# The second expert layer as seven block products in three of five chunks, and its weight sums on VectorE

## The chip, the cores and the metric

The kernel runs on one core of a Trainium2 chip. The metric is device time in microseconds (us) of one execution. The core has a matrix engine (TensorE, PE in the profile; its weight loads are shown as PEld), three engines for elementwise work (VectorE or DVE, ScalarE or ACT, GpSimd or POOL) and SyncE (SP), which only issues transfers here. Each engine works through its own instructions in the order in which they were written out. Semaphores make one engine wait for another. SBUF is the working memory; PSUM, in eight banks, takes what TensorE writes, and an elementwise engine has to move ("evacuate") it from there.

## The reference

Two layers in a row. The first is a Fourier filter on each of 8 batches of 2496 tokens by 256 channels, with a soft threshold:

```
X = rfft(x, axis=1);  Yr = Xr @ w_r - Xi @ w_i + b_r;  Yi = Xr @ w_i + Xi @ w_r + b_i
Y = sign(Y) * max(|Y| - 0.01, 0)          (for Yr and Yi)
y = irfft(Yr + i*Yi, n=2496, axis=1)
```

The second is a mixture of experts, in which the mean over the tokens of a batch picks one of 8 experts for the whole batch:

```
e = argmax(mean(y, axis=1) @ w_gate);  g = softmax weight of e
h   = relu(y @ w1[e])                     256 -> 1024 features
out = g * (h @ w2[e])                     1024 -> 256
```

Inputs and result are in 32 bits, the kernel's matmuls in 16 bits with sums in 32 bits.

## The kernel before

**Stages of a batch.** The transform of length 2496 is done in two factors (39 and 64) with matmuls against tables. For batches 2 to 7 the steps are: the first factor (L812), evacuated to `A`, stored to HBM as `fwd` and read back in another layout as `XB`; then, in five groups q of four frequencies each, the second factor (L876) to `XT`, a sum of real and imaginary part on VectorE (`sm`, L895), three products with the filter's weights (L914, `T2`, `T1`, `T0` in PSUM), and the threshold on VectorE; then the inverse's first factor (L547) from `Y` to `V`, stored to HBM as `scr` and read back as `V2`, and its second factor (L1058), evacuated to `ysb`, the expert layer's input. Batches 0 and 1 use a direct form (`add_attn_direct`).

**The threshold on VectorE** is, in each group q: two instructions that write `tt` = `T2` + bias, one for the real and one for the imaginary part (L928); two that write `z` = `T1` or `T0` + `tt` (L937); a clamp `cl` (L946); and four that write `Y` = `z` - `cl` (L956), each with two inputs in SBUF. L547 waits for all four.

**The expert layer** of a batch goes over five chunks of tokens: four of 512 and one of 448 (batch 0 has its own cut). In each chunk the first layer takes 8 x 2 matmuls of 512 columns (L1391), each pair evacuated with the relu to `hs` by ScalarE or VectorE (L1404, L1406). The second layer has two forms.
- *Plain* (L1440): for each of two tiles of 256 tokens 16 matmuls of 256 columns, 32 for a chunk; one evacuation of 512 elements for each tile, scaled by g, to `ost` (L1457 or L1460); a store.
- *Seven products* (`add_fast`, L1203): the chunk's 512 tokens are halved (t), and so are the 1024 features (k) and the 256 outputs (h). A product of two-by-two blocks, which takes eight block products, is made of seven block products (`p1` to `p7`), with sums of blocks before and after. Four sums of `hs` blocks go to `S`, or back into `hs` (L1221 to L1231, VectorE); four differences of `w2` blocks, `T`, are made once for each batch (L1193 to L1196, "weight sums"); each product is 8 matmuls of 128 columns (L1254), 56 in all. They build up in two PSUM banks, `E` and `F`. Between the products four evacuations of 256 elements take what `E` holds (`take`, L1269 on ScalarE or L1272 on VectorE), and three instructions on VectorE add what `F` holds to an `ost` block (`add`, L1278). `S` has one buffer, `hs` two, `T` one, `ost` four. `p5`, `p6`, `p7` and `p4` read `T[0]` to `T[3]`.

A set `FAST` (L394) says which chunks take the second form: four chunks of the last batch, and the fourth chunk of batches 1 to 6. The weight sums run on POOL for batches 1 to 6 and on VectorE for batch 7. The last chunk, of 448 tokens, has a second part with turned operands (L1325) and stores issued by POOL (L1362).

**What sets the order.** The kernel registers operations with a planner (`Schedule`, L136): an engine, a planned occupation and latency in us, a due time, what they depend on, which buffers they take. `run` (L197) then writes them out one by one: of those that could start it picks the one with the earliest planned start, then the earliest due time. Evacuations (`S.evac`) may go to ScalarE or VectorE, whichever the plan has free first. So a change of one operation's engine or length changes the order of all engines behind it, and the order is fixed before the kernel runs. TensorE gets work of two batches mixed: the expert layer of batch b beside the filter of batch b + 1 or b + 2.

**Queues.** SP issues the stores and the transfers over HBM; POOL issues the loads of the inputs (`xin`, L306 and L310) and of the chosen expert's weights (`w1s` L1150, `w2s` L1155, two buffers each), in its own order with the weight sums.

Of the kernel before, what the change touches and what calls it, by code (L numbers as in the profile page):

```python
# [10 lines left out]
FP16 = mybir.dt.float16  # L11
# [5 lines left out]
P = 128  # L17
B = 8
N = 2496
D = 256  # L20
E = 8
F = 1024
# [226 lines left out]
def kernel(  # L249
# [12 lines left out]
    nc = tc.nc  # L262
# [8 lines left out]
    def pool(name, bufs, **kw):  # L271
        return ctx.enter_context(tc.tile_pool(name=name, bufs=bufs, **kw))
# [21 lines left out]
    spool = pool("sp", 1)  # L294
# [72 lines left out]
    bias = cpool.tile([P, 2, D], FP32, name="bias")  # L367
# [17 lines left out]
    S = Schedule(BANKS)  # L385
    xin_t, V2_t, ysb_t, A_t, XB_t, fwd_t, scr_t = ({} for _ in range(7))
    gbc_t, w1s_t, w2s_t = {}, {}, {}
# [3 lines left out]
    W_LATE, B_LATE = 46.0, 53.5  # L391
    WARM, COLD, WARM_END = 60, 12, 11.9
    LATE = -0.12
    FAST = {(B - 1, c) for c in range(4)} | {(b, c) for b in range(1, B - 1) for c in (3,)}  # L394
    PERIOD, SPAN, SHIFT = 49.5, 1.4, 0.6

    ps = psum.tile([P, 8, 512], FP32, name="ps")
# [2 lines left out]
    def bank(tag):  # L400
        return ps[:, BASE[tag] + S.bank[tag]]
# [75 lines left out]
    c1, c2, c3 = ([S.fixed(t)] for t in X0_AT[1:])  # L477
# [319 lines left out]
    def add_attn(b):  # L797

        vt = vt_of(b)
# [4 lines left out]
        for gp in range(NG // 2):  # L804
            tk = S.tok("a", BANKS["a"])
            cell = {}

            def mm(_, gp=gp, cell=cell):
                if gp == 0:
# [6 lines left out]
                     deps=[xd[min(gp // 4, len(xd) - 1)]],  # L816
                     after=m if gp else None,
                     allocs=[tk] if gp else [tk, Ak])
# [11 lines left out]
        for i, (g0, g1) in enumerate(((0, 6), (6, 12), (12, 18), (18, 21))):  # L830
            def wr_(_, g0=g0, g1=g1):
# [6 lines left out]
                if g1 == 21:  # L838
# [5 lines left out]
                              deps=a_ops[g0 // 2 : (g1 + 1) // 2],  # L844
# [4 lines left out]
        for q in range(NQ):  # L849
            def rd(_, q=q):  # L850
                if b not in XB_t:
# [4 lines left out]
                              allocs=[] if q else [Bk]))  # L856

        v_ops = []
        for q in range(NQ):
            f = 0.1 + 0.7 * q / NQ  # L860
            cell = {}
# [3 lines left out]
            for ch in range(2):  # L865
                tk = S.tok("a", BANKS["a"])
                hc = {}

                def mm(_, q=q, ch=ch, cell=cell, hc=hc):
# [4 lines left out]
                    for i in range(4):  # L874
# [5 lines left out]
                         allocs=[tk] if ch else [tk, Xk])  # L880
# [19 lines left out]
            m_ops, toks = {}, {}  # L900
            zk, Yk = S.tok("z", BUFS["z"]), S.tok("Y", BUFS["z"])
            for t in (2, 1, 0):
                tk = S.tok("a", BANKS["a"])
                toks[t] = tk

                def mm(_, t=t, cell=cell):
# [5 lines left out]
                    for a in range(2):  # L912
                        for ch in range(2):
# [7 lines left out]
                                deps=([so] if t == 2 else [m_ops[2]]) + w_in + [w_late],  # L921
                                allocs=[tk, zk, Yk] if t == 2 else [tk])
                Xk.rel.append(m_ops[t])

            z_ops = []
            for r in range(2):
                def t1(_, r=r, cell=cell):
                    nc.vector.tensor_add(  # L928
                        out=cell["tt"][:, r], in0=cell["T", 2].rearrange(
                            "p (a c) -> p a c", a=2),  # L930
                        in1=bias[:, r].unsqueeze(1).to_broadcast([P, 2, D]))
                o1 = S.op("DVE", 0.61, t1, vt(f + 0.03), deps=[m_ops[2]],
                          lat=0.74)
                toks[2].rel.append(o1)

                def z_(_, r=r, cell=cell):
                    nc.vector.tensor_add(  # L937
                        out=cell["z"][:, r], in0=cell["T", 1 - r].rearrange(
                            "p (a c) -> p a c", a=2), in1=cell["tt"][:, r])
                o2 = S.op("DVE", 0.61, z_, vt(f + 0.03), lat=0.74,  # L940
                          deps=[o1, m_ops[1 - r]])
                toks[1 - r].rel.append(o2)
                z_ops.append(o2)
# [242 lines left out]
    def add_weight_sums(b, w, wk, v):  # L1186
        tk = S.tok("T", 1)

        def ts(_):
            T_t[b] = T = spool.tile([P, 4, 4, P], FP16, name="T")  # L1190
            w2 = w2s_t[b].rearrange("p (k i) (h c) -> p k h i c", k=2, h=2)
            sub = (nc.gpsimd if b < B - 1 else nc.vector).tensor_sub
            sub(out=T[:, 0], in0=w2[:, 0, 1], in1=w2[:, 0, 0])  # L1193
            sub(out=T[:, 1], in0=w2[:, 1, 1], in1=T[:, 0])
            sub(out=T[:, 2], in0=w2[:, 1, 1], in1=w2[:, 0, 1])
            sub(out=T[:, 3], in0=w2[:, 1, 0], in1=T[:, 1])  # L1196
        p = b < B - 1
        t = S.op("POOL" if p else "DVE", 4.5 if p else 1.4, ts, v, deps=[w],
                 lat=4.7 if p else 1.5, allocs=[tk])
        wk.rel.append(t)  # L1200
        return t, tk

    def add_fast(b, c, ns, nl, cell, h_ops, hk, wk, tt, gb_op, v0):  # L1203
        t_op, t_tok = tt
        th, m = nl // 2, nl // 4
        tag = "o" if b < B - 1 else "ho"[c % 2]
        sk = S.tok("S", 1)
# [2 lines left out]
        vt = lambda x: v0 + PERIOD * (c * 8 + 8 + x) / 44  # L1210
# [22 lines left out]
        o1 = s_op("s1", 0, s1, vt(0), h_ops, [sk])  # L1233
        o2 = s_op("s2", 0, s2, vt(0.1), [o1])
        o3 = s_op("s3", 0, s3, vt(0.2), [o1])
# [8 lines left out]
        w2 = lambda k, h: lambda f: w2s_t[b][:, 4 * k + f, P * h : P * h + P]  # L1244
        T = lambda i: lambda f: T_t[b][:, i, f]

        def prod(x, dst, a, bb, start, deps, allocs=(), after=None):
            def mm(_):
                if start:
                    fc[dst[0]] = bank(tag).rearrange(  # L1250
                        "p (h i c) -> p h i c", h=2, i=2)
                for t in range(2):
                    for f in range(4):
                        nc.tensor.matmul(  # L1254
                            fc[dst[0]][0:m, dst[1], t, :], A[a](f, t), bb(f),
                            start=start and t == 0 and f == 0,
                            stop=f == 3,
                            skip_group_check=True)
            return S.mm([P] * 8, mm, vt(x), deps=deps, allocs=allocs, after=after)
# [23 lines left out]
        p1 = prod(0, ("E", 0), "11", w2(0, 0), True, h_ops[:4], [ek])  # L1283
        c1 = take(0.1, 0, 0, [p1, gb_op])
        p2 = prod(1.2, ("F", 0), "12", w2(1, 0), True, h_ops, [fk], p1)
        p5 = prod(2.4, ("F", 1), "S1", T(0), False, [o1, t_op], after=p2)
        a11 = add(2.5, 0, 0, 0, [p5, c1])
        p6 = prod(3.6, ("E", 0), "S2", T(1), False, [o2, c1], after=p5)
        u2 = take(3.7, 0, 1, [p6])
        p7 = prod(4.8, ("E", 0), "S3", T(2), False, [o3, u2], after=p6)  # L1290
        u3 = take(4.9, 1, 1, [p7])
        a22 = add(5.0, 1, 1, 1, [u3, p5, a11])
        p4 = prod(6.0, ("E", 0), "22", T(3), False, [u3], after=p7)
        c21 = take(6.1, 1, 0, [p4])
        p3 = prod(7.2, ("F", 1), "S4", w2(1, 1), False, [o4, a22], after=p4)
        a12 = add(7.3, 0, 1, 1, [p3, u2])
# [14 lines left out]
    T_t = {}  # L1311
# [56 lines left out]
    def add_moe(b, y_ops, yk, gate):  # L1368
        w, gb_op, wk = gate
        v0 = b * PERIOD  # L1370
        if any(x == b for x, _ in FAST):
            t_op = add_weight_sums(b, w, wk, v0 - 0.05 * PERIOD)
        for c, (ns, nl, tiles) in enumerate(NCH0 if b == 0 else NCH):
            x = ns / 64
            hk = S.tok("hs", BUFS["hs"])
            cell = {}
            h_ops = []
            for fc in range(E):
                v = v0 + PERIOD * (x + fc * nl / 512) / 44
                tag = "h" if b < B - 1 else "a"  # L1380
                tk = S.tok(tag, BANKS[tag])
                hc = {}

                def mm(_, fc=fc, ns=ns, nl=nl, cell=cell, hc=hc, tag=tag):
                    if fc == 0:
                        cell["hs"] = hpool.tile([P, E, 512], FP16, name="hs")
                    hc["p"] = ph = bank(tag)

                    w1v = w1s_t[b].rearrange("p h (t f i) -> p h t f i", t=2, i=4)
                    for ch in range(2):  # L1390
                        nc.tensor.matmul(  # L1391
                            ph[:, 0:nl], w1v[:, ch, fc // 4, :, fc % 4],
                            ysb_t[b][:, ch, ns : ns + nl],
                            start=(ch == 0), stop=(ch == 1))
                need = y_ops[: Y_NEED[ns // YB]] if b == 0 else y_ops
                m = S.mm([nl, nl], mm, v, deps=need + [w], after=m if fc else None,
                         allocs=[tk] if fc else [tk, hk])
                yk.rel.append(m)
                wk.rel.append(m)

                def ev(eng, fc=fc, nl=nl, cell=cell, hc=hc):
                    o, i = cell["hs"][:, fc, 0:nl], hc["p"][:, 0:nl]
                    if eng == "ACT":
                        nc.scalar.activation(out=o, in_=i, func=AFT.Relu)  # L1404
                    else:
                        nc.vector.tensor_scalar_max(out=o, in0=i, scalar1=0.0)  # L1406
                e = S.evac(nl, ev, v, deps=[m])
                tk.rel.append(e)
                h_ops.append(e)
            if (b, c) in FAST:  # L1410
                add_fast(b, c, ns, nl, cell, h_ops, hk, wk, t_op, gb_op, v0)
                continue
            for sp, tile_s in enumerate(tiles):
# [11 lines left out]
                for q in range(4):  # L1425
                    if q // 2 >= tile_s[1]:
                        break
                    v = v0 + PERIOD * (x + 6 * nl / 512 + 4 * sp + q) / 44

                    def mm(_, tile_s=tile_s, q=q, cell=cell, oc=oc, tag=tago,  # L1430
# [8 lines left out]
                        for ft in range(4 * (q % 2), 4 * (q % 2) + 4):  # L1439
# [6 lines left out]
                             deps=h_ops[: 4 + 4 * (q % 2)],  # L1446
                             after=m2 if q else None,
                             allocs=[ok] if q == 0 else [ok2]
# [97 lines left out]
```

## Time and profile before

| what | us |
|---|---|
| median of 3 runs (452.35, 455.02, 454.74) | 454.74 |
| the profiled execution, one of these | 452.35 |
| its span, first to last instruction | 450.7 |
| TensorE busy | 422.8 |
| VectorE busy | 334.3 |
| ScalarE busy | 341.9 |
| POOL busy | 90.7 |
| first matmuls of the plain second layer (L1440) | 43.4 |
| first and last matmul of a seven-product chunk (L1254) | 134.7 and 443.4 |
| mean granted TensorE clock, as a share of full speed | 0.985 |

The page shows one execution. Busy time is the union of an engine's instructions; matmuls overlap, and their ends are modelled, so what a stream of them costs is read from the time between starts, or from the chain's pieces of many back-to-back matmuls. A group's mean is the length of one instruction; elementwise instructions that follow each other overlap by some 0.08 us, so that the time from start to start is that much shorter. "Idle before" is the time in which the engine stood still ahead of such instructions, with what ended it. A row of a window gives its length, then busy time and number of instructions of each engine, the granted TensorE clock, the mean busy share of the 16 DMA engines and GB/s.

From about 96 us on the batches run at an even pace: the same instructions come back each 54.4 to 54.5 us until 368 us, where the filter of the last batch runs out and the expert layers of batches 6 and 7 are left.

### The profile page before, as it was taken

The numbers are of one execution on the slowest core, as the hardware profiler recorded it, in microseconds if no ns is written. First come the engines' busy times: TensorE is split into PE (matmuls) and PEld (weight loads), VectorE is DVE, ScalarE is ACT, GpSimd is POOL, SyncE is SP. The second block draws the span as 40 slices with busy tenths as digits, with TensorE's granted clock in tenths as the row PEclk, the third lists the DMA queues.
The fourth block names the chain that finished last, engine by engine and source line by source line (L and its number), as shares of the span: only waits on it lengthen the run. The fifth ranks groups of instructions, "written<-read, shape, count | busy, mean of one in ns | idle before, by whom it ended". The sixth has DMA issues, their size and how long they took to land.

```text
span 450.7 us, 9985 instructions
## 1 busy us (share of the span) xinstructions
PE 422.8 (94%) x3745; PEld 320.9 (71%) x3745; DVE 334.3 (74%) x664; ACT 341.9 (76%) x679; POOL 90.7 (20%) x128
## 2 busy tenths in 40 slices
PE   5889999999999799988999799997999979999996
PEld 2567778886778677776677577776777767777775
DVE  1697875779679796796968968789877979536652
ACT  3788988878769587786867678675876958788884
POOL 5453140000013510144002530035200052000100
PEclk9999999999999899998999989999999989999999
DMA  7899799649859588587885788956987249432213
GB/s 141 215 181 173 131 285 218 181 109 207 235 202 176 126 184 246 185 182 134 212 250 165 154 169 214 283 119 134 219 225 238 86 74 203 143 119 77 61 70 111
DMA packets 70824, 76.99 MB, mean 171 GB/s; under 512 B 7128, under 2 KB 43696, under 8 KB 70776
## 3 DMA queue, kind: packets, MB, share of 16 engines
q1 hardware_dynamic: 57810, 56.23, 42.4%
q0 software_dynamic: 12704, 19.88, 28.1%
q8 instruction: 29, 0.48, 0.4%
q10 hardware_dynamic: 262, 0.25, 0.2%
q14 instruction: 19, 0.16, 0.1%
HBM read 57.54 MB, written 37.49 MB: 211 GB/s over the span
## 4 chain that ended last, share of the span: by engine, by line
PE 84%; DVE 9%; DMA 2%; issue 2%; ACT 1%; POOL 0%; DVEq 0%; SPq 0%; POOLq 0%
PE ps L1391 29%; PE ps L1440 20%; PE ps L914 9%; PE ps L1254 5%; DVE Y L956 5%; PE ps L547 4%; PE ps L718 4%; PE ps L812 3%; PE ps L1058 3%; PE ps L876 3%; PE ps L1325 2%; DMA xin<-in_x_dram 1%; DVE z L937 1%; PE ps L751 1%; PE ps L754 1%
## 5 line engine op out<-in xcount | busy, mean ns | idle before, releaser
L1404 ACT ACTIVATE hs<-ps 128x512 f16<-128x512 f32 (+3 forms) x317 | 177.5, 580 | 52.6 <-PE ps L1391 49.7
L1391 PE MATMUL ps<-ysb,w1s 128*128 128x512 f16 (+3 forms) x688 | 181.3, 359 | 0.1
L1440 PE MATMUL ps<-w2s,hs 128*128 128x256 f16 x864 | 123.4, 273 | 0.0
L1440 PEld LDWEIGHTS <-hs 128*128 128x128 f16 x864 | 83.7, 98 | 30.9 <-issue 0.9
L1391 PEld LDWEIGHTS <-w1s 128*128 128x128 f16 x688 | 72.3, 113 | 18.6 <-issue 0.7
L956 DVE TENSOR_TENSOR Y<-z,cl 64x512 f16<-64x512 f16 x120 | 67.4, 561 | 2.7
L914 PE MATMUL ps<-w,XT 128*128 128x256 f16 x360 | 49.9, 273 | 0.1
L928 DVE TENSOR_TENSOR tt<-ps,bias 128x512 f16<-128x512 f32 x60 | 38.6, 685 | 14.1 <-PE ps L914 13.9
L914 PEld LDWEIGHTS <-XT 128*128 128x128 f16 x360 | 35.0, 98 | 10.4 <-DVE XT L895 1.1
L1074 ACT CAST ysb<-ps 128x468 f16<-128x468 f32 (+1 forms) x63 | 33.5, 564 | 9.7 <-PE ps L1058 9.6
L554 ACT CAST V<-ps 128x512 f16<-128x512 f32 x47 | 27.8, 601 | 16.8 <-PE ps L547 16.3
L937 DVE TENSOR_TENSOR z<-ps,tt 128x512 f16<-128x512 f32 x60 | 38.7, 682 | 0.2
L547 PE MATMUL ps<-Y,ti 128*128 128x256 f16 x140 | 24.1, 275 | 14.9 <-DVE Y L956 14.9
L1457 ACT ACTIVATE ost<-ps,gbc 128x512 f32<-128x512 f32 (+1 forms) x45 | 30.2, 672 | 3.0 <-PE ps L1440 1.9
L547 PEld LDWEIGHTS <-ti 128*128 128x128 f16 x140 | 13.2, 98 | 22.0 <-issue 16.4
L822 ACT CAST A<-ps 120x512 f16<-120x512 f32 x46 | 26.0, 613 | 3.1 <-PE ps L812 3.1
L1058 PE MATMUL ps<-wi,V 120*128 120x117 f16 (+1 forms) x308 | 26.6, 225 | 0.0
L1254 PEld LDWEIGHTS <-hs 128*128 128x128 f16 x320 | 20.9, 98 | 6.3 <-ACT ost L1269 1.2
L319 POOL COPY xin<-V 1x2 f16<-1x2 f16 x4 | 0.8, 192 | 121.6 <-DMA V<-scr 121.6
L884 ACT CAST XT<-ps 128x512 f16<-128x512 f32 x41 | 24.7, 606 | 0.0
L1058 PEld LDWEIGHTS <-V 120*128 120x128 f16 x308 | 22.1, 104 | 2.8
L884 DVE CAST XT<-ps 128x512 f16<-128x512 f32 x19 | 13.1, 688 | 13.8 <-PE ps L876 13.0
(117 smaller groups left out, 601.8 us busy)
## 6 DMA issues: line engine op xcount, KB each, us to landing
out_dram<-ost SPq DMA_DIRECT2D x71, 256.0 KB
scr<-V SPq DMA_DIRECT2D x35, 256.0 KB
xin<-in_x_dram POOLq DMA_DIRECT2D x21, 390.0 KB, 9.8
XB<-fwd SPq DMA_DIRECT2D x30, 256.0 KB
V<-scr SPq DMA_DIRECT2D x14, 504.0 KB
fwd<-A SPq DMA_DIRECT2D x18, 360.0 KB
w1s<-in_moe_w_dram POOLq DMA_DIRECT2D x8, 512.0 KB, 6.7
w2s<-in_moe_w_dram POOLq DMA_DIRECT2D x8, 512.0 KB, 7.9
```

Of the source, the lines that this page charges most:

```text
L547: nc.tensor.matmul(pv[:, D * i : D * i + D], ti[:, 4 * q + k, :], cell["Y"](k))
L884: COPY[eng](out=cell["X"][:, ch, :, 0:2].rearrange("p a r i k -> p a i r k"), in_=hc["p"].rearrange("p (a i r k) -> p a i r k", a=2, i=2, ...
L914: nc.tensor.matmul(pm[:, D * a : D * a + D], cell["X"][:, ch, a, t].rearrange("p i k -> p (i k)"), w4[:, ch, t, :], start=(ch == 0), stop= ...
L928: nc.vector.tensor_add(out=cell["tt"][:, r], in0=cell["T", 2].rearrange("p (a c) -> p a c", a=2), in1=bias[:, r].unsqueeze(1).to_broadcast ...
L937: nc.vector.tensor_add(out=cell["z"][:, r], in0=cell["T", 1 - r].rearrange("p (a c) -> p a c", a=2), in1=cell["tt"][:, r])
L956: nc.vector.tensor_sub(out=Y[64 * r : 64 * r + 64, :, i], in0=cell["z"][s, r], in1=cell["cl"][s, r])
L1058: nc.tensor.matmul(pi[:, 117 * i : 117 * i + M], V2[:, g, ch * P : ch * P + P], w)
L1074: COPY[eng](out=yv[:, :, 12 * gb : 12 * gb + 3 * nf].rearrange("p a (g j) -> p a g j", j=3), in_=pi[:, 0 : 117 * nf].rearrange("p (g a j) ...
L1254: nc.tensor.matmul(fc[dst[0]][0:m, dst[1], t, :], A[a](f, t), bb(f), start=start and t == 0 and f == 0, stop=f == 3, skip_group_check=True)
L1391: nc.tensor.matmul(ph[:, 0:nl], w1v[:, ch, fc // 4, :, fc % 4], ysb_t[b][:, ch, ns : ns + nl], start=(ch == 0), stop=(ch == 1))
L1404: nc.scalar.activation(out=o, in_=i, func=AFT.Relu)
L1440: nc.tensor.matmul(oc["p"][:, i, :], cell["hs"][:, ft, ts], w2s_t[b][:, ft, :], start=(ft == 0), stop=(ft == E - 1))
```

## The change

Four edits.
1. `FAST` takes chunks 1, 2 and 3 of batches 1 to 6 in place of chunk 3 alone: twelve more chunks in the form with seven products.
2. The weight sums are on VectorE for every batch, as four operations of their own, and each product waits for the one that it reads, where all four were one operation.
3. In batches 1 to 6 the first of them is not written out ahead of the first evacuation of chunk 0 (`t_first.after`).
4. The two `tt` instructions become one of 1024 elements, with `T2` and the bias both broadcast.

```diff
-    FAST = {(B - 1, c) for c in range(4)} | {(b, c) for b in range(1, B - 1) for c in (3,)}
+    FAST = {(B - 1, c) for c in range(4)} | {(b, c) for b in range(1, B - 1) for c in (1,2,3,)}
...
+            def t1(_, cell=cell):
+                nc.vector.tensor_add(
+                    out=cell["tt"], in0=cell["T", 2].rearrange(
+                        "p (a c) -> p a c", a=2).unsqueeze(1).to_broadcast(
+                        [P, 2, 2, D]),
+                    in1=bias.unsqueeze(2).to_broadcast([P, 2, 2, D]))
+            o1 = S.op("DVE", 1.14, t1, vt(f + 0.03), deps=[m_ops[2]],
+                      lat=1.27)
+            toks[2].rel.append(o1)
             for r in range(2):
-                def t1(_, r=r, cell=cell):
-                    nc.vector.tensor_add(
-                        out=cell["tt"][:, r], in0=cell["T", 2].rearrange(
-                            "p (a c) -> p a c", a=2),
-                        in1=bias[:, r].unsqueeze(1).to_broadcast([P, 2, D]))
-                o1 = S.op("DVE", 0.61, t1, vt(f + 0.03), deps=[m_ops[2]],
-                          lat=0.74)
-                toks[2].rel.append(o1)
...
-        def ts(_):
-            T_t[b] = T = spool.tile([P, 4, 4, P], FP16, name="T")
-            w2 = w2s_t[b].rearrange("p (k i) (h c) -> p k h i c", k=2, h=2)
-            sub = (nc.gpsimd if b < B - 1 else nc.vector).tensor_sub
-            sub(out=T[:, 0], in0=w2[:, 0, 1], in1=w2[:, 0, 0])
-            sub(out=T[:, 1], in0=w2[:, 1, 1], in1=T[:, 0])
-            sub(out=T[:, 2], in0=w2[:, 1, 1], in1=w2[:, 0, 1])
-            sub(out=T[:, 3], in0=w2[:, 1, 0], in1=T[:, 1])
-        p = b < B - 1
-        t = S.op("POOL" if p else "DVE", 4.5 if p else 1.4, ts, v, deps=[w],
-                 lat=4.7 if p else 1.5, allocs=[tk])
-        wk.rel.append(t)
-        return t, tk
+        t_ops = []
+        for i in (0, 1, 2, 3):
+            def ts(_, i=i):
+                if i == 0:
+                    T_t[b] = spool.tile([P, 4, 4, P], FP16, name="T")
+                T = T_t[b]
+                w2 = w2s_t[b].rearrange("p (k i) (h c) -> p k h i c", k=2, h=2)
+                x, y = ((w2[:, 0, 1], w2[:, 0, 0]), (w2[:, 1, 1], T[:, 0]),
+                        (w2[:, 1, 1], w2[:, 0, 1]), (w2[:, 1, 0], T[:, 1]))[i]
+                nc.vector.tensor_sub(out=T[:, i], in0=x, in1=y)
+            t = S.op("DVE", 0.35, ts, v, deps=[w] + t_ops[-1:], lat=0.48,
+                     allocs=[] if i else [tk])
+            wk.rel.append(t)
+            t_ops.append(t)
+        return t_ops, tk
...
-        p5 = prod(2.4, ("F", 1), "S1", T(0), False, [o1, t_op], after=p2)
+        p5 = prod(2.4, ("F", 1), "S1", T(0), False, [o1, t0], after=p2)
...
-        p6 = prod(3.6, ("E", 0), "S2", T(1), False, [o2, c1], after=p5)
+        p6 = prod(3.6, ("E", 0), "S2", T(1), False, [o2, c1, t1_], after=p5)
...
+            if c == 0 and 0 < b < B - 1:
+                t_first.after = h_ops[0]
```

`p7` and `p4` get `t2` and `t3` in the same way.

More of the change, by code (lines that the diff above doesn't have):

```diff
@@ L1187, in add_weight_sums @@
         tk = S.tok("T", 1)
-        def ts(_):
-            T_t[b] = T = spool.tile([P, 4, 4, P], FP16, name="T")
-            w2 = w2s_t[b].rearrange("p (k i) (h c) -> p k h i c", k=2, h=2)
-            sub = (nc.gpsimd if b < B - 1 else nc.vector).tensor_sub
[L1193 to L1196, printed above, removed]
-        p = b < B - 1
-        t = S.op("POOL" if p else "DVE", 4.5 if p else 1.4, ts, v, deps=[w],
-                 lat=4.7 if p else 1.5, allocs=[tk])
-        wk.rel.append(t)
-        return t, tk
+        t_ops = []
[13 more added lines that the diff above has]
+        return t_ops, tk
     def add_fast(b, c, ns, nl, cell, h_ops, hk, wk, tt, gb_op, v0):
-        t_op, t_tok = tt
+        (t0, t1_, t2, t3), t_tok = tt
         th, m = nl // 2, nl // 4
@@ L1285, in add_fast @@
         p2 = prod(1.2, ("F", 0), "12", w2(1, 0), True, h_ops, [fk], p1)
-        p5 = prod(2.4, ("F", 1), "S1", T(0), False, [o1, t_op], after=p2)
+        p5 = prod(2.4, ("F", 1), "S1", T(0), False, [o1, t0], after=p2)
         a11 = add(2.5, 0, 0, 0, [p5, c1])
-        p6 = prod(3.6, ("E", 0), "S2", T(1), False, [o2, c1], after=p5)
+        p6 = prod(3.6, ("E", 0), "S2", T(1), False, [o2, c1, t1_], after=p5)
         u2 = take(3.7, 0, 1, [p6])
-        p7 = prod(4.8, ("E", 0), "S3", T(2), False, [o3, u2], after=p6)
+        p7 = prod(4.8, ("E", 0), "S3", T(2), False, [o3, u2, t2], after=p6)
         u3 = take(4.9, 1, 1, [p7])
         a22 = add(5.0, 1, 1, 1, [u3, p5, a11])
-        p4 = prod(6.0, ("E", 0), "22", T(3), False, [u3], after=p7)
+        p4 = prod(6.0, ("E", 0), "22", T(3), False, [u3, t3], after=p7)
         c21 = take(6.1, 1, 0, [p4])
@@ L1372, in add_moe @@
             t_op = add_weight_sums(b, w, wk, v0 - 0.05 * PERIOD)
+            t_first = t_op[0][0]
         for c, (ns, nl, tiles) in enumerate(NCH0 if b == 0 else NCH):
```

## The prediction

> **What bounds the kernel now.** I read the page first: its head, the busy time of each engine and the chain of work that ended last.
>
> ```profile
> span 450.7 us, 9985 instructions
> PE 422.8 (94%) x3745; PEld 320.9 (71%) x3745; DVE 334.3 (74%) x664; ACT 341.9 (76%) x679; POOL 90.7 (20%) x128
> PE 84%; DVE 9%; DMA 2%; issue 2%; ACT 1%; POOL 0%; DVEq 0%; SPq 0%; POOLq 0%
> ```
>
> TensorE is busy 94% of the span and carries 84% of the chain; VectorE carries 9%. Next, the list of who waited for whom on TensorE (us in total, times, longest). After the start-up one entry is large:
>
> ```profile
> PE ps L547 <- DVE Y L956: 14.9, 10, 2.0
> ```
>
> Ten waits, two in each of five batches, for the subtraction that writes Y. The timeline shows why (start, length, engine, line). The first row is a usual group of four Y instructions, the rest a group that has POOL's weight sums beside it:
>
> ```profile
> 106.53 1.74 DVE L956 TENSOR_TENSOR Y<-z,cl 64x512 f16<-64x512 f16 x4
> ...
> 144.71 1.34 POOL L1193 TENSOR_TENSOR T<-w2s 128x512 f16<-128x512 f16 x1 [7.46 <-PE ps L1254]
> 145.07 5.14 DVE L956 TENSOR_TENSOR Y<-z,cl 64x512 f16<-64x512 f16 x4
> 146.13 1.21 POOL L1194 TENSOR_TENSOR T<-w2s,T 128x512 f16<-128x512 f16 x1
> 147.31 1.33 POOL L1195 TENSOR_TENSOR T<-w2s 128x512 f16<-128x512 f16 x1
> 148.60 1.33 POOL L1196 TENSOR_TENSOR T<-w2s,T 128x512 f16<-128x512 f16 x1
> 148.97 0.27 PE L547 MATMUL ps<-Y,ti 128*128 128x256 f16 x1 [1.96 <-DVE Y L956]
> 150.26 0.49 PE L547 MATMUL ps<-Y,ti 128*128 128x256 f16 x3 [1.02 <-DVE Y L956]
> ```
>
> Four Y instructions take 1.74 us alone and 5.14 us beside POOL: while POOL subtracts from SBUF to SBUF, each Y instruction (two SBUF inputs) ends only as the next POOL instruction does. The 3.4 us lost become 1.96 + 1.02 = 3.0 us of idle TensorE. This comes back at 199, 254, 308 and 361 us. A second price follows at once. Two rows by windows (length, busy time and count of PE, PEld, DVE, ACT and POOL, then granted clock, DMA share, GB/s):
>
> ```profile
> 150.50:154.80 4.30, 4.30 (x41) 4.09 (x39) 2.09 (x5) 2.98 (x7) 0.15 (x1) 0.60 0.65 100
> 150.50:205.00 54.50, 51.51 (x446) 39.35 (x444) 44.40 (x86) 40.34 (x81) 12.78 (x18) 0.97 0.77 189
> ```
>
> In the 4.3 us after the wait the granted clock is 0.60: 4.3 x 0.40 = 1.7 us. The same dip follows four of the five waits (0.68 over 204.9 to 210.2, 0.66 over 259.3 to 264.3, 0.62 over 366.0 to 370.5); outside it the clock is full. In the rest of a batch TensorE goes without a gap of note. A batch from 150 to 368 us takes 54.4 to 54.5 us, and that is TensorE's work plus this stall. VectorE idles 54.5 - 44.4 = 10.1 us of it.
>
> **The change, part by part**, against the profiled execution (452.35 us, its span 450.7 and 1.65 around it).
>
> *Seven products instead of 32 matmuls*, in 12 more chunks (two in each of batches 1 to 6). The chain gives both forms, back to back at full clock:
>
> ```profile
> 408.71 0.89 PE ps L1254 x16
> ...
> 410.02 1.75 PE ps L1440 x16
> ```
>
> A 128-column matmul takes 0.89/16 = 56 ns, a 256-column one 1.75/16 = 109 ns. A chunk goes from 32 x 109 = 3.50 us to 56 x 56 = 3.13 us: 0.36 us saved, 12 x 0.36 = **4.3 us**. That the halved width stays hidden behind the weight loads is read here, not assumed: each of these matmuls has its own load. In the trace's fast chunks the 56 ns hold whenever eight follow each other.
>
> The Trainium skill speaks against this part: "TensorE: Matmul & The Clock Gate", section "Back-to-back issue gap", puts sustained pairs of load and matmul at about 81 ns for 128 columns and 131 ns for 512. By an estimate from that page (some 98 ns at 256 columns) a chunk would go from 3.1 to 4.5 us, and the part would cost 17 us instead of saving 4. The rows above differ from it, so they decide.
>
> *Weight sums from POOL to VectorE.* POOL loses four subtractions in each of batches 1 to 6, so nothing is left on it that slows Y after the start. The waits go: **14.9 us**. The clock dips that follow them go: four of 1.7, of which I take 1.5 each since the windows hold some idle time: **6 us**. On VectorE the sums cost 1.55 us per batch, as measured in batch 7 (four instructions, 409.29 to 410.84). They are due behind the first evacuation of chunk 0, need weights that landed most of a batch earlier, and the first product that reads them comes a chunk later, so no matmul waits for them by itself. What stands behind the sums in POOL's queue moves up: the next w1s load, which went out at 149.87 right after the sums, can go some 5 us earlier, where DMA is quiet (share 0.18 over 146 to 150.5). w2s still waits for its buffer. I price that at nothing.
>
> *Bias step merged.* Two instructions of 0.61 us each, start to start, become one of 1024 elements. No row shows that form. Between two of the present ones (1.21, no gain) and one fixed part less (1142 ns start to start for a 1024-element evacuation), I take 1.15: 5 x 0.06 = 0.3 us of VectorE per batch. The first z now waits for all of it, 0.5 us later, but the second comes no later.
>
> *VectorE's new load.* For each converted chunk four S sums and three adds. In the profile's groups:
>
> ```profile
> L1278 DVE SCALAR_TENSOR_TENSOR ost<-ps,gbc,ost 128x256 f32<-128x256 f32 x30 | 14.4, 480 | 11.4 <-ACT ost L1269 8.4 <-PE ps L1254 2.8
> L1221 DVE TENSOR_TENSOR S<-hs 128x1024 f16<-128x1024 f16 x10 | 6.9, 688 | 0.4
> L1231 DVE TENSOR_TENSOR S<-hs,S 128x1024 f16<-128x1024 f16 x10 | 6.8, 685 | 0.0
> ```
>
> Four S sums took 2.6 us in a row (403.66 to 406.27); an add is 0.40 us start to start, 0.48 alone. Per batch, from the 44.4 us of the window above: Y unblocked, 11.8 to 8.7, -3.1; S sums 2 x 2.6 = +5.2; adds 6 x 0.44 = +2.6; weight sums +1.55; bias -0.3. In the changed program's instruction order VectorE also gives up 20 evacuations, about four per batch, x 0.65 = -2.6. Sum: **47.8 us**. TensorE's own batch becomes 54.5 - 3.0 - 1.5 - 0.7 = **49.3 us**. So VectorE would be 97% busy in a batch TensorE could finish in 49.3. ScalarE takes eight more 256-element evacuations (0.36 us start to start), about four fewer 512-element output ones (0.57) and three other ones (0.48): 40.3 + 2.9 - 2.3 + 1.4 = 42.3 us, 86%, no bound.
>
> Here lies the unknown: how much VectorE, working in order, still waits in those 1.5 us of room. In the changed order the three fast chunks follow each other, and between the Y groups of one batch VectorE's work by these durations is 10.9, 9.9, 9.6, 4.5 and 11.5 us against 10.9, 10.2, 9.7, 4.6 and 13.1 us of matmuls. Four of the five stretches have no slack, so any wait in them ends on TensorE. From below the price is 0 (the 1.5 us suffice). From above it is 8.6 us per batch, if VectorE keeps its 10.1 us of idle time; but that is mostly waiting for TensorE, which a full engine does not do (tt for L914 is 13.9 us of it over the run). I take 1.5 us per batch, nearer the low end: 5 x 1.5 = **7.5 us** of new stalls, in pieces too short to lower the clock.
>
> Sum: 452.35 - 4.3 - 14.9 - 6 + 7.5 = 434.7. The median of the three runs is 454.74, the profiled one the fastest of them by 2.4. As I rounded the stall and clock terms down (in start-to-start gaps the five waits are 3.3 us each, 16.5), I leave the spread out and forecast **434 us**.
>
> **Rivals.**
> *TensorE stays the only bound.* VectorE's 1.5 us of room is enough, and stalls vanish: 434.7 - 7.5 = 427 us. For it: before, TensorE has no gap outside the Y wait. Against: VectorE had 10 us of slack then.
> *VectorE sets the pace.* It keeps half of its idle time, 5 us: a batch is 52.8 us, 3.5 over 49.3, so 427.2 + 5 x 3.5 = 445 us. For it: four stretches without slack, and a fast chunk's takes, adds and products alternate between three engines on two PSUM banks (the trace's took 189.2 to 199.7, 10.5 us). Against: the order puts other instructions between dependent ones.
> *Slower than before, by the same queue.* VectorE keeps over 6.7 us of its idle time. 427.2 + 5 x 5.2 = 453 is where the gain ends, a batch of 54.5. At 8 us kept it is 427.2 + 5 x 6.5 = 460. It needs VectorE to wait as much as when it was not the bound; little speaks for that.
> *DMA binds.* The share of 0.77 to 0.80 becomes about 0.85 in a shorter batch. The first 96 us already run at 0.84 with the first transfers alone waited for, so this is part of the second rival.
>
> **How the numbers follow.** Forecast (430 to 439) 0.55; TensorE alone (425 to 430) 0.17; VectorE's pace (439 to 449) 0.2; within 1% of before 0.03; slower 0.05. 1% is about what a measurement of this kernel can tell from no change. Faster by over 1% is 0.92. The range 425 to 445 leaves out the slow cases and half of the second rival's far end.
>
> **What would show it.** POOL without L1193 to L1196; Y groups of 1.74 us throughout; no wait of L547 over 1 us; granted clock 0.99 or more in the windows after 150 us; VectorE near 48 us per batch of about 50.8; new small waits of TensorE for S, ost, Y or XT. Wrong would be: Y groups still stretched (then POOL was not the cause), 128-column matmuls over 60 ns in the new chunks, or VectorE idle over 5 us in a batch with TensorE waiting for it.

## The result and the profile after

The changed kernel takes 430.81 us (median of four runs, 429.83 to 432.09) against 453.55 for the kernel before (now four runs, 452.11 to 455.02): a ratio of 0.950, 95% interval 0.945 to 0.955. It is faster by 5%; the forecast was 434 us, 3 us more. The profiled execution took 432.09 us, its span 430.4.

The head of the page of the changed kernel, with the busy time of each engine, and its chain by engine:

```profile
span 430.4 us, 10644 instructions
PE 414.7 (96%) x4033; PEld 314.8 (73%) x4033; DVE 351.8 (82%) x722; ACT 354.0 (82%) x723; POOL 61.0 (14%) x104
PE 80%; DMA 9%; ACT 4%; DVE 4%; issue 1%; POOL 1%; DVEq 0%; POOLq 0%
```

TensorE is busy for 8 us less and for a larger share; VectorE has 17.5 us more work. The head of the list of who waited for whom on TensorE (us in total, times, longest):

```profile
PE ps L457 <- ACT warm L350: 3.4, 1, 3.4
PE ps L1059 <- DMA V<-scr: 1.5, 1, 1.5
PE ps L674 <- DMA xin<-in_x_dram: 1.3, 1, 1.3
PE ps L592 <- DVE Y L781: 0.9, 2, 0.7
PE ps L718 <- ACT w L409: 0.8, 1, 0.8
PE ps L914 <- DVE XT L895: 0.8, 2, 0.5
```

The entry of 14.9 us, L547 waiting for Y, is gone. Most of what is left belongs to the start; new is one wait of 1.5 us for the read of `scr` in batch 1. New too is DMA's 9% of the chain: the round trip over `scr` ahead of that wait is 10.3 us of it, three output stores are 20.9 us. The first of these stores in the chain, and in the timeline what stood behind it:

```profile
195.22 6.99 DMA out_dram<-ost
...
202.30 0.58 DVE L1353 STREAM_TRANSPOSE ost<-ost 128x384 f32<-128x384 f32 x1 [0.65 <-DMA out_dram<-ost]
...
202.80 0.38 DVE L895 TENSOR_TENSOR XT<-XT 128x512 f16<-128x512 f16 x1
...
203.24 0.61 PE L914 MATMUL ps<-w,XT 128*128 128x256 f16 x4 [0.31 <-DVE XT L895]
```

The transposition (L1353) on VectorE waits for the store to free one of the four `ost` buffers, the `XT` sum stands behind it in VectorE's order, and TensorE waits for the sum. This happens in three batches; TensorE lost 0.3 us here and 0.5 us in one more, the last entry shown of its list. VectorE's timeline and group rows show the Y instructions, the sums that are now VectorE's own, and the new forms (group rows: busy us, mean ns of one, idle before):

```profile
145.34 1.29 DVE L938 TENSOR_TENSOR z<-ps,tt 128x512 f16<-128x512 f32 x2
...
146.94 0.42 DVE L947 TENSOR_SCALAR cl<-z 128x1024 f16<-128x1024 f16 x1
147.39 1.74 DVE L957 TENSOR_TENSOR Y<-z,cl 64x512 f16<-64x512 f16 x4
...
152.87 0.41 DVE L1199 TENSOR_TENSOR T<-w2s 128x512 f16<-128x512 f16 x1
```

```profile
L957 DVE TENSOR_TENSOR Y<-z,cl 64x512 f16<-64x512 f16 x120 | 50.3, 419 | 2.4
...
L928 DVE TENSOR_TENSOR tt<-ps,bias 128x1024 f16<-128x1024 f32 x30 | 36.6, 1219 | 2.6 <-PE ps L914 1.8 <-DMA V<-scr 0.7
```

All 120 Y instructions take 50.3 us; before it was 67.4:

```profile
L956 DVE TENSOR_TENSOR Y<-z,cl 64x512 f16<-64x512 f16 x120 | 67.4, 561 | 2.7
```

By windows, one batch each (length, then PE, PEld, DVE, ACT and POOL busy and counts, granted clock, DMA share, GB/s):

```profile
147.00:196.80 49.80, 49.58 (x495) 38.00 (x494) 46.23 (x96) 42.77 (x90) 7.69 (x13) 1.00 0.86 208
196.80:246.70 49.90, 49.37 (x490) 37.44 (x489) 45.69 (x94) 42.45 (x89) 7.58 (x13) 1.00 0.83 205
246.70:296.50 49.80, 49.52 (x492) 37.58 (x489) 45.84 (x95) 42.57 (x89) 7.80 (x13) 1.00 0.83 205
```

A batch takes about 49.8 to 50 us instead of 54.5, at full clock; VectorE is busy for 46 of it. The products hold the rate of the trace before (chain of waits):

```profile
179.15 0.89 PE ps L1257 x16
...
185.07 0.89 PE ps L1257 x16
```

### The profile page after: what moved, and what is told of

Its sections match the earlier page's. It is cut to its first block, busy times and chain, and to the rows that moved or that the text cites. A ratio compares the mean times of both kernels' runs of the same rounds, so it can differ in the third digit from the quotient of the medians.

```text
span 430.4 us, 10644 instructions
## 1 busy us (share of the span) xinstructions
PE 414.7 (96%) x4033; PEld 314.8 (73%) x4033; DVE 351.8 (82%) x722; ACT 354.0 (82%) x723; POOL 61.0 (14%) x104
## 4 chain that ended last, share of the span: by engine, by line
PE 80%; DMA 9%; ACT 4%; DVE 4%; issue 1%; POOL 1%; DVEq 0%; POOLq 0%
PE ps L1395 29%; PE ps L1257 15%; PE ps L1446 10%; PE ps L914 8%; DMA out_dram<-ost 5%; PE ps L812 3%; PE ps L547 3%; PE ps L718 3%; PE ps L876 2%; PE ps L1059 2%; DMA scr<-V 2%; ACT hs L1408 2%; DMA xin<-in_x_dram 1%; DVE z L766 1%; PE ps L1328 1%
## 5 line engine op out<-in xcount | busy, mean ns | idle before, releaser
L1446 PE MATMUL ps<-w2s,hs 128*128 128x256 f16 x480 | 69.5, 272 | 0.0
L1446 PEld LDWEIGHTS <-hs 128*128 128x128 f16 x480 | 45.6, 98 | 14.0 <-issue 0.2
L1257 PEld LDWEIGHTS <-hs 128*128 128x128 f16 x704 | 46.1, 98 | 12.8
L957 DVE TENSOR_TENSOR Y<-z,cl 64x512 f16<-64x512 f16 x120 | 50.3, 419 | 2.4
L914 PE MATMUL ps<-w,XT 128*128 128x256 f16 x360 | 50.3, 273 | 0.9 <-DVE XT L895 0.8
L1272 ACT ACTIVATE ost<-ps,gbc 128x256 f32<-128x256 f32 x88 | 42.8, 487 | 2.9 <-PE ps L1257 2.6
L1281 DVE SCALAR_TENSOR_TENSOR ost<-ps,gbc,ost 128x256 f32<-128x256 f32 x66 | 31.1, 479 | 14.7 <-ACT ost L1272 10.4
L1257 PEld LDWEIGHTS <-S 128*128 128x128 f16 x528 | 34.3, 98 | 11.0 <-DVE S L1224 1.6
L914 PEld LDWEIGHTS <-XT 128*128 128x128 f16 x360 | 33.4, 98 | 10.9 <-DVE XT L895 3.0
L928 DVE TENSOR_TENSOR tt<-ps,bias 128x1024 f16<-128x1024 f32 x30 | 36.6, 1219 | 2.6 <-PE ps L914 1.8
L1257 PE MATMUL ps<-T,S 128*128 128x128 f16 x352 | 26.9, 219 | 0.2
L1257 PE MATMUL ps<-T,hs 128*128 128x128 f16 x352 | 26.8, 219 | 0.0
L1257 PE MATMUL ps<-w2s,hs 128*128 128x128 f16 x352 | 26.0, 219 | 0.0
```

Source lines behind the costliest of these rows:

```text
L914: nc.tensor.matmul(pm[:, D * a : D * a + D], cell["X"][:, ch, a, t].rearrange("p i k -> p (i k)"), w4[:, ch, t, :], start=(ch == 0), stop= ...
L928: nc.vector.tensor_add(out=cell["tt"], in0=cell["T", 2].rearrange("p (a c) -> p a c", a=2).unsqueeze(1).to_broadcast([P, 2, 2, D]), in1=bi ...
L957: nc.vector.tensor_sub(out=Y[64 * r : 64 * r + 64, :, i], in0=cell["z"][s, r], in1=cell["cl"][s, r])
L1257: nc.tensor.matmul(fc[dst[0]][0:m, dst[1], t, :], A[a](f, t), bb(f), start=start and t == 0 and f == 0, stop=f == 3, skip_group_check=True)
L1272: nc.scalar.activation(out=ost(t, h), in_=src, func=AFT.Copy, scale=gbc_t[b][0:m])
L1281: nc.vector.scalar_tensor_tensor(out=ost(t, h), in0=fc["F"][0:m, half], scalar=gbc_t[b][0:m], in1=ost(t, h), op0=ALU.mult, op1=ALU.add)
```

## The experiments

Two theories stood against each other first. *Theory:* POOL, reading SBUF for the weight sums, holds up the Y instructions; moving the sums is nearly all of the gain. *Rival:* the seven products and the denser order make it. Afterwards the question was what sets the rest of TensorE's losses.

The table gathers what the traces show over four batches, from the fifth Y group to the twenty-fifth. "Lost" is the time between starts of matmuls beyond what the same matmuls take back to back (56 ns for 128 columns, 109 for 256 and so on), lowered clock included; it is good to about 0.15 us. These three columns are of the one traced execution of each kernel; each ratio is to the kernel before on the same chip (453.55 to 453.70 us).

| kernel | median us | ratio to before | us per batch | lost per batch | VectorE busy per batch |
|---|---|---|---|---|---|
| before | 453.6 | 1 | 54.1 | 5.0 | 44.3 |
| changed (again) | 430.5 | 0.949 | 49.8 | 1.5 | 46.0 |
| e1: before, sums on VectorE | 432.6 | 0.954 | 50.6 | 1.5 | 41.9 |
| e2: changed, old chunks | 431.9 | 0.951 | 50.2 | 1.1 | 40.9 |
| e5: changed, chunks 2 and 3 | 431.0 | 0.950 | 49.8 | 1.2 | 43.6 |
| e3: changed, sums on POOL | 448.4 | 0.989 | 53.1 | 4.8 | 47.9 |
| e4: changed, two bias steps | 434.4 | 0.960 | 50.6 | 2.2 | 47.2 |
| e6: before, POOL only writes | 429.3 | one run | 49.5 | 0.5 | 40.9 |
| e7: changed, measured lengths in the plan | 433.7 | 0.957 | 50.3 | 2.0 | 46.6 |
| e8: changed, copies for S sums | 428.2 | 0.945 | 49.6 | 1.3 | 43.2 |
| e9: changed, clamp twice | 442.0 | 0.977 | 51.6 | 3.3 | 48.0 |
| e10: e2, clamp twice | 441.7 | 0.975 | 51.6 | 2.5 | 43.0 |
| e11: changed, evacuations moved to ScalarE | 433.3 | 0.957 | 49.7 | 1.4 | 44.5 |

**The changed kernel again**, as the measure of e1, e2 and e5, which ran on the same chip.

> The changed kernel again, on the same chip as the next three, as their measure. Both theories: 430 to 432 us, ratio 0.95 to before.

Measured: 430.46 us, 0.949 (0.947 to 0.951).

**Weight sums alone.** Every other edit is left out; the planner makes the order anew.

```diff
-            sub = (nc.gpsimd if b < B - 1 else nc.vector).tensor_sub
+            sub = nc.vector.tensor_sub
...
-        p = b < B - 1
+        p = False
```

> The kernel before with one edit: the weight sums of batches 1 to 6 on VectorE, in one operation. Theory (POOL's reads hold up Y): the five waits and the clock dips behind them go, 453.6 - 14.9 - 6.8 = 432 us, Y groups of 1.74 us. Rival (the gain is that of the seven products and of the denser order): at least 450 us.

Measured: 432.55 us, 0.954 (0.951 to 0.956). This one edit is 21.1 us of the 23.2 us that the changed kernel gained on the same chip. The rival falls.

**Sums undone in the changed kernel.** They are one operation on POOL again, and the products that read them wait for all of it.

```diff
-            t = S.op("DVE", 0.35, ts, v, deps=[w] + t_ops[-1:], lat=0.48, ...
+        t = S.op("POOL" if p else "DVE", 4.5 if p else 1.4, ts, v, deps=[w], ...
...
-            if c == 0 and 0 < b < B - 1:
-                t_first.after = h_ops[0]
```

> The changed kernel with one edit undone: the weight sums of batches 1 to 6 on POOL again, at their old place. Theory (POOL's reads hold up Y, 3.3 us of waiting and up to 1.7 us of lowered clock in each of five batches, and VectorE now has no slack to catch up): 430.8 + 16 to 25 = 447 to 456 us, Y groups stretched to about 5 us beside the sums. Rival (the place of the sums is worth little): under 434 us.

Measured: 448.44 us, 0.989 (0.985 to 0.992), 18 us more than the changed kernel. TensorE's wait for Y is back in its list of waits:

```profile
PE ps L547 <- DVE Y L957: 11.5, 11, 1.8
```

And its timeline shows both sides of it, one Y group beside the sums of batch 3:

```profile
199.75 1.15 POOL L1194 TENSOR_TENSOR T<-w2s 128x512 f16<-128x512 f16 x1 [5.92 <-PE ps L1255]
...
199.98 1.29 DVE L938 TENSOR_TENSOR z<-ps,tt 128x512 f16<-128x512 f32 x2
...
200.99 1.16 POOL L1195 TENSOR_TENSOR T<-w2s,T 128x512 f16<-128x512 f16 x1
...
201.58 0.85 DVE L947 TENSOR_SCALAR cl<-z 128x1024 f16<-128x1024 f16 x1
...
202.10 1.34 POOL L1196 TENSOR_TENSOR T<-w2s 128x512 f16<-128x512 f16 x1
202.46 3.44 DVE L957 TENSOR_TENSOR Y<-z,cl 64x512 f16<-64x512 f16 x4
...
203.40 1.33 POOL L1197 TENSOR_TENSOR T<-w2s,T 128x512 f16<-128x512 f16 x1
```

Two Y instructions fell beside POOL, hence 3.44 us. The z instructions (one input in SBUF, one in PSUM) keep their 1.29 us beside POOL's first subtraction and the start of its second; the clamp, one input in SBUF, takes 0.85 instead of 0.42.

**POOL writes, but does not read.** The kernel before, in its own order; the weight sums of batches 1 to 6 are left out.

```diff
+            if b < B - 1:
+                for i in range(4):
+                    for _r in range(3):
+                        nc.gpsimd.memset(T[:, i], 0.0)
+                return
             sub(out=T[:, 0], in0=w2[:, 0, 1], in1=w2[:, 0, 0])
...
```

> The kernel before with POOL's weight sums of batches 1 to 6 replaced by twelve instructions that only write zeros to the same tile, so that the sums are left out. If POOL's reading of SBUF is what holds up an instruction of VectorE with two SBUF inputs, Y groups beside them take 1.74 us and the kernel 432 us or a little less. If any work of POOL on SBUF does it, Y groups are stretched there by several of these instructions and L547 waits again.

Measured: 429.3 us in one run, and in its timeline:

```profile
144.51 6.86 POOL L1196 MEMSET T<- 128x512 f16 x12 [7.81 <-PE ps L1259]
...
144.89 1.74 DVE L956 TENSOR_TENSOR Y<-z,cl 64x512 f16<-64x512 f16 x4
...
146.66 0.60 PE L547 MATMUL ps<-Y,ti 128*128 128x256 f16 x4
```

POOL works for 6.9 us on the same tile at the same place, and the whole Y group passes beside it in 1.74 us. So it is POOL's reading that collides, not its being busy or its writes. The Trainium skill states this rule: "SBUF — State Buffer", section "Who interferes with whom", says that a VectorE instruction with two SBUF inputs contends with a GpSimd instruction that reads SBUF and not with one that only writes. These runs agree on both halves. This run also shows what is lost in a batch when no engine carries the sums: 0.5 us.

**The twelve chunks undone**, and, in a kernel of its own, one chunk of the three in each batch.

```diff
-    ... for c in (1,2,3,)}
+    ... for c in (3,)}            (e2)
+    ... for c in (2,3,)}          (e5)
```

> The changed kernel with the old set of chunks, so that weight sums and bias step alone are changed. Theory: the twelve chunks are worth 4.3 us of matmuls less the new stalls. With stalls of 7.5 us as forecast this kernel is faster than the changed one, 428 us; with the stalls of the changed kernel's trace (some 5 us more than without) it is level with it, 430 to 432 us. Rival (the seven products make the gain): 447 us or more.

> The changed kernel with chunks 2 and 3 instead of 1, 2 and 3 in batches 1 to 6. If VectorE is the bound with three chunks, one chunk less takes 3.7 us of its work from each batch and the stalls shrink by more than the 0.36 us of matmuls added: 427 to 430 us. If TensorE still is the bound, it is slower by 6 x 0.36 = 2.2 us: 433 us.

Measured: 431.86 (0.951, interval 0.949 to 0.954) and 431.01 us (0.950, 0.947 to 0.952). The twelve chunks are worth 1.4 us by the medians, and the intervals overlap. Of the first expectation the second case holds (level, 430 to 432), not the one with stalls of 7.5 us. Back to back, the matmuls of a batch do go from 49.06 to 48.33 us, the 0.73 forecast; but the loss per batch goes from 1.1 to 1.5 (the products' own waits, for `S` and for the adds, from 0.05 to 0.38), and at the start the read of `scr` is waited for 1.2 us instead of 0.7. Neither sentence of the second expectation holds: the middle version is level.

**The bias step undone.**

```diff
-                    out=cell["tt"], ... .to_broadcast([P, 2, 2, D])
+                    out=cell["tt"][:, r], ... .to_broadcast([P, 2, D])    (twice, 0.61 us each in the plan)
```

> The changed kernel with the bias step as two instructions again. Theory: VectorE has 0.07 us more work in each of 30 groups, most of them in stretches without slack: 430.8 + 1 to 2 = 432 to 433 us. Rival (it is hidden, or the earlier first z is worth more): 429 to 431 us.

Measured: 434.42 us, 0.960 (0.957 to 0.962), 4 us more than the changed kernel. The merged step takes 1134 ns from start to start against 2 x 602 in this kernel, so 30 x 0.07 = 2.1 us of the 4 are explained if all of that comes out. The order, which the planner makes anew, is another cause (lost per batch 2.2 instead of 1.5, with TensorE waiting for `A`, z and `ost`). How the 4 us divide between the two was not taken apart.

**Truer lengths in the plan.**

```diff
-            oy = S.op("DVE", 1.5, y_, vt(f + 0.03), deps=[oc_], lat=1.62)
+            oy = S.op("DVE", 1.74, y_, vt(f + 0.03), deps=[oc_], lat=1.80)
...
-            return S.op("DVE", 0.36, ad, vt(x), deps=deps, lat=0.5)
+            return S.op("DVE", 0.40, ad, vt(x), deps=deps, lat=0.54)
...
+            o.occ["ACT"], o.lat["ACT"] = 0.36, 0.50       (take)
```

> The changed kernel with three of the planner's lengths set to what the trace shows (Y group 1.74 instead of 1.50 us, add 0.40 instead of 0.36, a 256-element evacuation on ScalarE 0.36 instead of 0.29). If the stalls left come from a plan that counts VectorE some 1.6 us too short for each batch, they shrink: 427 to 429 us. If they come from VectorE's work itself, 430 to 432 us.

Measured: 433.71 us (0.957), slower than the changed kernel and than both forecasts. The new order lets TensorE wait for the `XT` sum (L914, 5.3 us in five waits). A truer plan for three operations is not a better order here.

**How much of what is left is VectorE's load.** Two kernels in the changed kernel's own order, one with less work on VectorE, one with more, and the latter also in e2, whose VectorE has 9 us of slack in a batch. In the first the S sums are left out.

```diff
-            nc.vector.tensor_add(out=fc["S"][:, 0, :, 0:th], in0=hv(0, 1), in1=hv(1, 1))
+            nc.vector.tensor_copy(out=fc["S"][:, 0, :, 0:th], in_=hv(1, 1))     (e8; S2 to S4 likewise)
...
+                for _i in range(2):                                              (e9, e10)
                     nc.vector.tensor_scalar(
                         out=cell["cl"], in0=cell["z"], scalar1=-LAM, scalar2=LAM,
```

> The changed kernel in its own order, with the four S sums of each seven-product chunk replaced by copies of one input to the same place, so that the sums are left out. A copy should take about 0.34 us instead of 0.60 (the clamp of 1024 elements, also one input in SBUF, does), 3 us less of VectorE's work for each of batches 1 to 6. Theory A (what TensorE still loses, 1.5 us a batch in start-to-start gaps, is VectorE's work without slack): 0.5 us a batch left, 425 to 427 us. Theory B (it is latency from engine to engine and the planned order): 429 to 431 us.

> The changed kernel in its own order, with the clamp of each of the 30 groups done twice, 0.34 us more of VectorE, 1.7 us a batch. Theory A: VectorE has no slack in four of five stretches, so most of it comes out: 30 x 0.34 x 0.6 to 0.9 = 6 to 9 us, 436 to 440 us. Theory B: 430 to 433 us.

> The same doubled clamp in the kernel with the old set of chunks, whose VectorE is busy 40.9 us of a batch of 50.2. Theory A: the work is hidden by 9 us of slack, 0 to 3 us, 432 to 435 us, clearly less than in the changed kernel. Theory B (the longer chain to Y is what costs): the same addition as in the changed kernel.

Measured: 428.19 (0.945, interval 0.942 to 0.949), 442.0 (0.977) and 441.73 us (0.975). Neither theory forecast all three. The copies lie between the two: taking 2.8 us of VectorE's work from each batch brings 0.3 us a batch, 2.3 us in all; the products' waits for `S` and for the adds are what goes, and the wait of 1.2 us for `scr`. The doubled clamp in the changed kernel cost more than either theory allowed. In e2's kernel theory A (VectorE has no slack and its work comes out) fails and theory B holds: adding 30 x 0.34 = 10.2 us costs 11.5 us where VectorE is busy 46 of 50 us, and 9.9 us where it is busy 41 of 50, the same within the spread of the runs, and about all of it. So VectorE's load in a batch does not set the price; what fits is where the work stands. The clamp is on the way to Y, and TensorE's list of waits of e10 shows it ahead of L547, in many small pieces:

```profile
PE ps L547 <- DVE Y L958: 3.3, 17, 0.2
...
PE ps L547 <- DVE z L938: 0.7, 3, 0.2
```

In gaps between starts, the time lost ahead of L547 for Y goes from 0.4 to 1.7 us a batch there, and from under 0.1 to 1.4 in e9. That L547 stands in TensorE's order where the plan expects Y, with nothing else to run behind it, is the reading that fits; a kernel with L547 placed later was not run.

**Evacuations moved to ScalarE.**

```diff
-PEN = 0.2
+PEN = 0.6
```

> The changed kernel with the planner's penalty for an evacuation on VectorE raised from 0.2 to 0.6 us: in its order some 15 large evacuations, 9 us, move from VectorE to ScalarE. Theory A: TensorE's remaining loss shrinks, 427 to 429 us, if ScalarE, then 45 us busy in a batch, bears it. Otherwise 430 us or more.

Measured: 433.32 us, 0.957 (0.954 to 0.960). VectorE is freed of 1.5 us a batch, the batch is level in the traced execution (49.7), the fastest of four with 431.03 us, and the median is 2.9 us longer than the changed kernel's. That fits e8, in that VectorE's load is not the bound, but shows less, since the planner made the order anew. No kernel that computes everything beat the changed one clear of noise.

## Why the prediction was right

**Weight sums, -14.9 and -6: right in cause, some 3 us too small in size.** Moved alone they gave 21.1 us (e1) against 20.9 in the sum. That agreement is in part luck: e1 loses 1.5 us a batch, 1.0 more than e6, with the sums' work on VectorE and a new order. With the sums on no engine 24.2 us came back (e6, one run). The clock is 1.00 in the windows after 150 us, where it dipped to 0.60 to 0.68. e6 settles what the prediction left open, whether POOL's being busy or its reading does it.

**Matmuls, -4.3: right.** 0.89 us for 16 in the new chunks, 0.73 us less per batch. The 81 ns of "TensorE: Matmul & The Clock Gate", "Back-to-back issue gap", that spoke against it do not hold here; these chunks ran at 56.

**New stalls, +7.5: this is the term that was mis-sized, and its reason was wrong.** The prediction started from 49.3 us per batch and added 1.5, 50.8 in all; the batch is 49.8. Half of the difference is the base: TensorE's own work is 48.33, and 0.5 us is lost even without the sums (e6), 48.8 together. The five waits are 3.3 us each between starts, not 3.0. The other half is the stalls: 1.0 us a batch beyond e6's 0.5, 5 us in five batches and not 7.5. Of the 1.0, 0.6 came with the sums and the bias step on VectorE (e2), 0.4 with the twelve chunks. And the reason, "any wait in them ends on TensorE" in stretches without slack, would make VectorE's load the price: e10, where the same addition costs as much with 9 us of slack, speaks against it, and e8 shows that 2.8 us less load takes away only 0.2 of the 1.5 us lost.

**VectorE's load, 47.8: too high by 1.8.** Measured 46.0. The added terms hold: from e2 to the changed kernel it rises by 5.1 us, where S sums, adds and evacuations given up came to 5.2. The base is off: with Y unblocked and nothing else changed (e6) a batch has 40.9, 3.4 less and not 3.1, and the kernel with sums and bias merged (e2) has 40.9 again where the working gives 42.5. ScalarE's 42.3 came to 42.6.

**Bias, 1.15 us for the merged form: right (1.134).** Its worth was not: undoing it costs 4 us, where 0.3 a batch had been put down, and part of that may be the order.

**The rivals.** The one that left TensorE the only bound (427 us) was nearly as good a description as the forecast: the result lies 0.8 us inside the near edge of the forecast's band. The terms of the sums (too small) and of the stalls (too large) err to the same side, and a traced run 1.2 us below the median of before hid part of that. That VectorE sets the pace (439 to 449 us), or loses the whole gain, is refuted by the time. DMA came to about the 0.85 expected (0.83 to 0.86 in the three windows above). In the even stretch the output stores shown above cost TensorE 0.3 and 0.5 us in the profiled execution, and 0.1 in e0; in batch 1 a read was waited for 1.2 to 1.5 us. Neither was forecast.

## What to carry to other kernels

When one group of instructions is at times three times as long as usual, look at what the other engines read at that moment: four instructions of POOL off the critical path, 5.2 us long, cost 4 to 5 us of TensorE time in each batch, wait and lowered clock together. In a kernel whose order is fixed, price an edit by the place of its instruction, not by the engine's total alone: here 0.34 us on the way to a matmul came out in full with 9 us of slack on its engine, while 2.8 us taken off elsewhere on the same engine brought 0.3. And fewer matmul columns were worth a third of their arithmetic here (1.4 of 4.3 us by the medians, not clear of noise); the sums that replace them bring waits of their own.

## What had not been expected

- The write-only form: twelve instructions of POOL, 6.9 us long in total, beside a Y group that still took 1.74 us.
- The clamp, with one SBUF input and its output in SBUF, took 0.85 us instead of 0.42 where it started beside a POOL subtraction (e3), while z (1.29 us for two) kept its length.
- Copies of 1024 elements took 0.42 to 0.43 us against 0.69 for the sums they replaced in e8.
